# A planned attention and feed-forward kernel: g as two rows, another first order of loads and squares, double score steps from pair 6

## The chip, the cores and the metric

The kernel runs on one NeuronCore of a Trainium2 chip. The metric is the device time of one execution in microseconds (us); lower is better. Before the change three runs gave 427.59, 427.06 and 425.68 us, median 427.06. The engines are called as in the profile: PE (TensorE, matmuls; PEld its weight loads), ACT (ScalarE), DVE (VectorE), POOL (GpSimd) and SP (SyncE, which here issues DMAs). A name with q, such as SPq, is the engine's instruction queue.

## The reference

Attention over 8 batches, 12 heads, 448 tokens and 64 columns a head, with q and k normalised, and behind it a gated feed-forward layer on all 3584 tokens:

```python
def rmsnorm(x, g):
    rms = np.sqrt(np.mean(x * x, axis=-1, keepdims=True) + 1e-06)
    return x / rms * g
q_n, k_n = (rmsnorm(q, g_q), rmsnorm(k, g_k))
scores = scale * np.matmul(q_n, k_n.transpose(0, 1, 3, 2))
attn = np.exp(scores - max); attn = attn / sum
x = np.matmul(attn, v), heads side by side          # 3584 x 768
h = x @ w_in                                        # 768 x 2048
out = (h * np.clip(h + 3.0, 0.0, 6.0) / 6.0) @ w_out  # 2048 x 768
```

## The kernel before

**Units of work.** Two heads make a pair: 6 pairs a batch, 48 in all (HP = 6, NPAIR = 48). A head's 448 tokens are three tiles of 128 and a rest of 64; the rests of a pair's two heads lie together in a fourth tile.

**The way of a pair.** Its q, k and v are loaded from HBM (`load_main`, `load_rest`) into `qk_st` and `v_st`. `square` (L373 on ACT, L375 on POOL) and `sums` (L378, DVE) give the sums of squares; `rstd` (L389, L391, ACT) turns them into the factor 1/rms by a logarithm and an exponential; `normalize` (L399 for pairs 0 to 3, L401 behind) multiplies q or k by it, on POOL, or on DVE for q of pairs 0 and 1 (`DN`), in which case the factor lies in a PSUM bank. Each of the two is then turned so that the 64 columns of a head lie on the partitions: by PE transposes (L418, L421, L425) up to pair 11, by a DMA from pair 12 on (TD). `put_k` (L351) and `put_q` (L439 on DVE, L437 on ACT) copy them into `qkT`; `put_q` multiplies by `gprime`, which holds g_q x g_k / 8 on 128 partitions. `make_g` (L596, L598, ACT) computes it from two loads of 64 numbers to 64 partitions (`load_g`, L592, issued on SP).

**Scores.** `score` (L448) has four steps a pair: three *half steps*, one for each full tile, in which each head's matmul uses one half of PE's rows (the profile shows 64*128, x2), and a *rest step* with one matmul over all rows. `expo` (L463, ACT) writes the exponentials into `eD` (half steps) and `eR` (rest step). `weigh` (L480) multiplies them with `vaug`, the bf16 v with a column of ones, into the bank `av`; `divide` (L490 to L499, DVE) divides by the sum, and `x_out` with `put_x` (L508 to L525) turns the result into `xT`, a batch's x with the 768 columns on partitions.

**Feed-forward.** For each batch `h_mm` (L528) makes 16 tiles of h, six matmuls each; `relu` (L534, ACT) and `gate` (L539, DVE) write `gT`; `y_mm` (L547) makes the output rows, `y_copy` (L351) brings them to SBUF and `y_store` out. w_in comes in eight blocks and w_out in four, one DMA each on POOL's queue (L363), as bf16.

**PSUM.** Eight banks: units 0 and 1 are two banks wide (`sc`, used for scores), 2, 3 and 4 one bank (`ps`), and one is `av`.

**Order.** Nothing is scheduled while it runs: a planner (class `Plan`) plays the kernel through before it is built, and writes out each engine's instructions in the order in which it began them. An operation (`add`) has a key (lower goes first), one or more ways (engine and estimated ns), and what it depends on. Where there are several ways, the estimate is multiplied by a price for its engine (`FIRST` before 45 us, `PRICE` behind). DMAs have an estimated size and landing, with `SLOW`, `BEGIN`, `LATE` and `AHEAD` as allowances, and at most eight are under way. PE takes attention work first, except where a running credit, fed by `share`, hands it to feed-forward items. The engines then work strictly in that order, so an instruction that waits holds up all behind it on its engine.

**What the prediction touches.** The first DMAs: k of pair 0 on SP, q of pairs 0 and 1 on ACT, then the two g loads, k of pair 1, k and q of pairs 2, 3, all on SP; behind them v of pairs 0, 1, v of 2, 3, then k, q and v of 4, 5. The first weight block waits for v of 2, 3. `steps` issues score steps; below pair PB = 12 each by itself, from there on two half steps together (a double), which needs both units 0 and 1. Loads of pairs below MB = 12 (`dense` rows, seven tokens to a partition) take two DMAs, those behind one. `hold` is a one-element memset on POOL that keeps a load back until an earlier pair is normalised.

Of the kernel before, what the change touches and what calls it, by code (L numbers as in the profile page):

```python
# [26 lines left out]
class Op:  # L27


    def __init__(self, key, ways, deps, lag=0, size=0, want=None, cell=None):  # L30
        self.key, self.ways, self.lag, self.size = key, ways, lag, size
        self.want, self.cell, self.gives, self.calm = want, cell, [], None
# [12 lines left out]
class Plan:  # L45
# [8 lines left out]
    UNITS = 5  # L54

    def __init__(self, share):
        self.free = {e: 0.0 for e in ("PE", "ACT", "DVE", "POOL", "SP")}
        self.known, self.todo = [], 0
# [5 lines left out]
    def add(self, key, ways, deps=(), lag=0, size=0, hold=False, want=None, cell=None):  # L64
        op = Op(key, ways, deps, lag, size, want, cell)
        op.left += hold
        op.subs = 0
# [15 lines left out]
    def item(self, lane, place, count, ns, fn, deps, want):  # L83
# [6 lines left out]
        return it  # L90

# [62 lines left out]
    def begin(self, op, engine, ns, fn, now, banks):  # L154
        if banks is not None:
            op.cell["b"] = banks
            for b in banks:
                self.users[b] = list(op.gives)
# [15 lines left out]
    def run(self):  # L174
        now = 0.0
        while self.todo or self.row or any(self.lanes.values()):
            self.flow(now)
            soon = [t for t in self.free.values() if t > now]
# [5 lines left out]
            best = {}  # L184
            for op in self.known:
# [3 lines left out]
                if op.calm is not None and (self.backlog("SP", "ACT") > op.calm[0] + 3000 or self.backlog("POOL") > op.calm[1]):  # L189
                    continue  # L190
                engine, ns, fn = min(op.ways, key=lambda w: max(self.free[w[0]], now) + w[1] * ((self.FIRST if now < self.UNTIL else self.PRICE).get(w[0], 1.0) if op.key[0] >= 0 else 1.0))
                if self.free[engine] <= now and (engine not in best or op.key < best[engine][0].key):
                    if op.subs and not self.room(op, engine, now):
                        continue
                    banks = self.banks_for(op, now, soon) if op.want else None
                    if op.want is None or banks is not None:
                        best[engine] = (op, ns, fn, banks)
            if self.free["PE"] <= now and ("PE" not in best or self.credit < 0):
                if self.row:
                    best["PE"] = (self.row[0], *self.row[0].ways[0][1:], None)  # L200
                else:
                    pick = self.next_item(now, soon)
                    if pick:
# [5 lines left out]
                        best["PE"] = (self.row[0], *self.row[0].ways[0][1:], banks)  # L209
            if not best:  # L210
                now = min(soon)
            for engine, (op, ns, fn, banks) in best.items():
# [5 lines left out]
                else:  # L218
                    self.known.remove(op)
# [8 lines left out]
def kernel(  # L228
# [32 lines left out]
    DENSE, PD, MB = 2 * NT + 1, 4, 12  # L261
# [10 lines left out]
    gq_t = const.tile([P, 1], FP32, name="gq_t")  # L272
    gk_t = const.tile([P, 1], FP32, name="gk_t")
# [30 lines left out]
    plan = Plan(share=(1.4, 1.0, 0.45, 3.0, 0.42, 5.0, 0.4))  # L304
# [139 lines left out]
    def score(p, i, u):  # L444

        qkT = qkT_r[p % NK]
        for h, rows in enumerate((lo, hi) if i < NT else (slice(0, P),)):
            nc.tensor.matmul(  # L448
                out=bank(u, h)[:, 0:S], lhsT=qkT[rows, 0, i * P:(i + 1) * P], rhs=qkT[rows, 1, 0:S],
# [3 lines left out]
    def expo(p, i, u):  # L453
# [4 lines left out]
        else:  # L458
            e, src = eD_t[:, (NT * p + i) % NED], unit_r[u]
            parts = ((e[:, 0:2 * FULL].rearrange("p (h c) -> p h c", h=2), src[:, :, 0:FULL]),  # L460
                     (e[:, 2 * FULL:].rearrange("p (n c) -> p n c", n=3)[:, 0:3:2], src[:, :, FULL:S]))
        for out, in_ in parts:
            nc.scalar.activation(out=out, in_=in_, func=EXP, bias=0.0, scale=1.0)  # L463

    def e_part(p, i, h, j):

        e = eR_t[:, p % NER] if i == NT else eD_t[:, (NT * p + i) % NED]
        heads = 1 if i == NT else 2
        c = h % heads * FULL + j * P if j < NT else heads * FULL + h * REST
# [115 lines left out]
    def clear_e(eng):  # L585
        eng.memset(none[:], 0.0)
        eng.memset(eR_t[:, :, S:W4], 0.0)
        eng.memset(eD_t[:, :, 2 * FULL + REST:2 * FULL + 2 * REST], 0.0)

    def load_g(eng):  # L590
        for dst, src in ((gq_t, g_q), (gk_t, g_k)):
            eng.dma_start(out=dst[lo, :], in_=src.rearrange("(p o) -> p o", o=1))  # L592
# [9 lines left out]
    NFAST = 12  # L602
    CALM = (3000, 100), (5000, 1000)
    SC, ANY = [(0,), (1,)], [(4,), (3,), (1,), (0,), (2,)]
# [7 lines left out]
    ff_banks = [(4,), (3,), (2,)]  # L612
# [27 lines left out]
    def h_item(b, f):  # L640
        deps = [w_ops[f * P // WC]] + px[HP * b:HP * b + HP]
        deps += y_ops.get(b - 2, [])[-1:] + (y_rest.get(b - 1, []) if b % 2 == 0 else [])
        it = plan.item("h", b + f / NFT, NKT, 189, lambda kt, m: h_mm(b, f, kt, m), deps, lambda: ff_banks)
# [3 lines left out]
    def h_early(f):  # L647
        cell, ops = {}, []
        for kt in range(NKT):
            ops.append(add((kt + 2, 2), [("PE", 189, lambda kt=kt: h_mm(0, f, kt, cell["b"][0]))],  # L650
                           [px[kt], at(ops, kt - 1), w_ops[f * P // WC]] + [px[HP - 2]] * (kt == 0), 165,
                           want=any_of((2,), (3,)) if kt == 0 else None, cell=cell))
# [3 lines left out]
    def y_item(b, t, c, n, place):  # L656
        part = c // YC
        deps = [*w_ops[NWI + part * NFT // WR:NWI + (part + 1) * NFT // WR], *gates[b], *(gates[b - 1] if t == NT else [])]
        it = plan.item("y", place, NFT, 163 * n // YC, lambda f, m: y_mm(b, t, c, n, f, m), deps, lambda: ff_banks)
# [35 lines left out]
    YLAG, EARLY = 0.3, 1  # L695

    W_AFTER, LA, VL = 2, 3, 1.2
    DN = ((0, 1), (1, 1))
    MG, EACH = 10, 0.5
    V0, V2, LATER, AHEAD = 2.5, 0.8, -1, 3000  # L700
# [20 lines left out]
    def clear_slots(p):  # L721

        op = add((p - 4, 4), [("POOL", 900, lambda: clear(G, slice(p % NS, p % NS + 2))),
# [19 lines left out]
    def hold(p):  # L743

        cell = qk_st[0:1, 0, p % NS, 0, 0, 0:1]
        held[p] = [add((0, p), [("POOL", 80, lambda: nc.gpsimd.memset(cell, 0.0))], norms[p - (4 if p < 18 else LA)] + norms.get(p - NS, []))]

    def load(a, p, main, rest, rank, aq=nc.sync, qq="SP"):
        if main:
            op = plan.dma((p + rank, a), 2 if PD * (a < 2) <= p < MB else 1, main * 560 * (1.13 if a < 2 and p < PD else 1), lambda: load_main(aq, a, p, main), slot_free(a, p, main) + held.get(p, []), queue=qq)  # L750
# [8 lines left out]
    def load_half(a, p, rest, half, rank, aq=nc.sync, qq="SP"):  # L759
        op = plan.dma((p + rank, a + 0.1), 1, rest * (280 if a == 1 else 140),  # L760
# [7 lines left out]
    def stats(p, st):  # L768
# [4 lines left out]
        srcs = [landed[0][p], landed[1][p]]  # L773
# [191 lines left out]
```

## Time and profile before

| | |
|---|---|
| Median of three runs | 427.06 us |
| Profiled execution, time | 427.18 us |
| Profiled execution, span from first to last instruction | 425.4 us |
| Granted TensorE clock, mean | 1.000 |
| Read from HBM, written | 45.61 MB, 11.01 MB |

| PE group | line | count | busy us | mean ns |
|---|---|---|---|---|
| h matmuls, 448 columns | L528 | 768 | 172.3 | 353 |
| y matmuls, 384 columns (and 192) | L547 | 912 | 169.1 | 323 |
| half steps, 64 rows | L448 | 288 | 43.7 | 361 |
| rest steps | L448 | 48 | 17.3 | 361 |
| weighing | L480 | 1392 | 86.9 | 194 to 223 |

A matmul's busy time runs on after the next one has begun, so the sums of the table overlap; what a matmul costs is read from the distance between starts. In the timeline each line is a start, a length, an engine, a line of the kernel and an operation, with neighbours of one kind merged (x6); behind it in brackets stands the idle time of the engine just before and what ended it. In the list of waits, each line names who waited for whom, the total, the count and the longest.

### The profile page before, as it was taken

How to read it: one execution, taken by the hardware profiler on the slowest of the kernel's cores; microseconds unless marked ns; L12 is line 12 of the kernel's file. 1: busy time of each engine (PE TensorE's matmuls, PEld its weight loads, DVE VectorE, ACT ScalarE, POOL GpSimd, SP SyncE). 2: the span in 40 equal slices, each digit the busy share in tenths (PEclk: the TensorE clock that was granted, in tenths of full speed). 3: DMA queues.
4: the chain of work that ended last, by engine and by line, in shares of the span. 5: the costliest groups of instructions: out<-in, count | busy, mean ns of one | idle time of the engine just before them, and what ended most of it. 6: DMA issues, size and time to landing. Idle time of an engine off the chain costs nothing.

```text
span 425.4 us, 9409 instructions
## 1 busy us (share of the span) xinstructions
PE 407.6 (96%) x3646; PEld 232.0 (55%) x3646; DVE 212.0 (50%) x434; ACT 291.3 (68%) x687; POOL 205.0 (48%) x220
## 2 busy tenths in 40 slices
PE   0888999999999999999999999999999999999996
PEld 0455565555565555555555555555556555555564
DVE  5666887627454565556535675464433432042100
ACT  4799988777868889888887897788663333243211
POOL 5889775773657685685675666784100000000000
PEclk9999999999999999999999999999999999999999
DMA  7999999998899999999499996973311300100121
GB/s 216 195 207 212 181 241 233 161 193 191 185 209 212 209 212 192 224 198 253 111 203 213 219 185 146 223 192 62 85 54 39 86 2 37 75 0 39 74 76 74
DMA packets 128285, 65.11 MB, mean 153 GB/s; under 512 B 78320, under 2 KB 124784, under 8 KB 128240
## 3 DMA queue, kind: packets, MB, share of 16 engines
q1 hardware_dynamic: 117520, 57.76, 63.5%
q0 software_dynamic: 10432, 6.29, 11.0%
q8 instruction: 28, 0.46, 0.5%
q10 hardware_dynamic: 288, 0.46, 0.3%
q14 instruction: 17, 0.14, 0.1%
HBM read 45.61 MB, written 11.01 MB: 133 GB/s over the span
## 4 chain that ended last, share of the span: by engine, by line
PE 91%; ACT 3%; DMA 2%; DVE 2%; SPq 1%; POOL 0%; issue 0%; ACTq 0%; POOLq 0%
PE ps L547 35%; PE ps L528 34%; PE av L480 11%; PE sc L448 10%; ACT eD L463 2%; DMA qk_st<-in_q_dram 2%; PE ps L425 1%; DVE ssq L378 1%; ACT eR L463 0%; PE ps L418 0%; ACT sq L373 0%; SPq L331 0%; DVE gT L539 0%; SPq L592 0%; DVE xn L496 0%
## 5 line engine op out<-in xcount | busy, mean ns | idle before, releaser
L528 PE MATMUL ps<-xT,w_in_sb 128*128 128x448 bf16 x768 | 172.3, 353 | 0.1
L547 PE MATMUL ps<-w_out_sb,gT 128*128 128x384 bf16 (+1 forms) x912 | 169.1, 323 | 0.0
L463 ACT ACTIVATE eD<-sc 128x768 bf16<-128x768 f32 (+1 forms) x288 | 137.1, 555 | 23.0 <-PE sc L448 20.3
L539 DVE SCALAR_TENSOR_TENSOR gT<-t_sb,ps 128x448 bf16<-128x448 f32 x128 | 79.0, 619 | 103.6 <-ACT t_sb L534 102.4
L401 POOL TENSOR_TENSOR qkn<-qk_st,rstd 128x512 bf16<-128x512 f32 x88 | 89.3, 1041 | 49.7 <-ACT rstd L391 47.2
L547 PEld LDWEIGHTS <-gT 128*128 128x128 bf16 x912 | 82.8, 98 | 53.8 <-issue 7.4
L528 PEld LDWEIGHTS <-w_in_sb 128*128 128x128 bf16 x768 | 68.1, 98 | 58.2 <-issue 9.9
L534 ACT ACTIVATE t_sb<-ps 128x448 f32<-128x448 f32 x128 | 70.6, 553 | 33.1 <-PE ps L528 30.3
L375 POOL TENSOR_TENSOR sq<-qk_st 128x1024 f32<-128x1024 f32 (+2 forms) x47 | 78.5, 1682 | 16.6 <-DMA qk_st<-in_q_dram 11.1
L480 PEld LDWEIGHTS <-eD 128*128 128x128 bf16 x1152 | 53.2, 98 | 22.7 <-issue 5.0
L448 PE MATMUL sc<-qkT 64*128 64x448 bf16 (+1 forms) x336 | 60.9, 361 | 2.9 <-ACT eD L463 2.2
L378 DVE TENSOR_REDUCE ssq<-sq 128x16 f32<-128x1024 f32 (+2 forms) x50 | 57.9, 1162 | 10.5 <-POOL sq L375 5.1
L480 PE MATMUL av<-vaug,eD 128*128 128x65 bf16 x1152 | 59.6, 194 | 0.0
L351 ACT COPY y_sb<-ps 128x384 f32<-128x384 f32 (+1 forms) x43 | 20.3, 472 | 55.2 <-PE ps L547 54.8
L351 POOL CAST vaug<-v_st 128x512 bf16<-128x512 f32 x32 | 19.6, 617 | 40.6 <-PE av L480 27.7
L463 ACT ACTIVATE eR<-sc 128x448 bf16<-128x448 f32 x96 | 31.8, 390 | 8.6 <-PE sc L448 8.4
L448 PEld LDWEIGHTS <-qkT 64*128 64x128 bf16 (+1 forms) x336 | 14.9, 94 | 29.1 <-issue 24.5
L437 ACT ACTIVATE qkT<-qkT,gprime 128x448 bf16<-128x448 bf16 x36 | 24.3, 676 | 0.5 <-DMA qkT<-qkn 0.5
L490 DVE RECIPROCAL rden<-av 128x7 f32<-128x7 f32 x48 | 9.7, 201 | 29.8 <-PE av L480 29.8
L496 DVE TENSOR_TENSOR xn<-av,rden 128x384 bf16<-128x384 f32 x42 | 23.4, 557 | 1.6 <-DVE rden L490 0.2
L351 DVE COPY y_sb<-ps 128x384 f32<-128x384 f32 x14 | 7.8, 557 | 27.9 <-PE ps L547 27.9
L480 PEld LDWEIGHTS <-eR 128*128 128x128 bf16 x240 | 16.5, 98 | 7.7 <-issue 2.6
(60 smaller groups left out, 146.5 us busy)
## 6 DMA issues: line engine op xcount, KB each, us to landing
qk_st<-in_k_dram SPq DMA_DIRECT2D x18, 384.0 KB, 4.0
qk_st<-in_q_dram SPq DMA_DIRECT2D x18, 384.0 KB, 4.8
v_st<-in_v_dram SPq DMA_DIRECT2D x18, 384.0 KB, 5.5
out_dram<-y_sb SPq DMA_DIRECT2D x17, 384.0 KB, 2.5
out_dram<-y_sb SPq DMA_DIRECT2D x21, 192.0 KB, 3.2
w_in_sb<-in_moe_w_in_dram POOLq DMA_DIRECT2D x8, 384.0 KB, 7.8
w_out_sb<-in_moe_w_out_dram POOLq DMA_DIRECT2D x4, 768.0 KB, 10.0
v_st<-in_v_dram SPq DMA_DIRECT2D x12, 192.0 KB, 7.8
```

Source lines behind the costliest of these rows:

```text
L351: (eng.copy if eng is nc.scalar else eng.tensor_copy)(out=out, in_=in_)
L375: eng.tensor_tensor(out=sq, in0=x, in1=x, op=A_MULT)
L378: nc.vector.tensor_reduce(out=packed(p, ssq_r[:, p % NR, a]), in_=packed(p, sq_r[m % 2][:, a]), axis=mybir.AxisListType.X, op=A_ADD,)
L401: eng.tensor_tensor(out=qkn_r[p % NQ][:, a].rearrange("p t h d -> p h t d"), in0=qk_st[:, a, p % NS], in1=by[:, a].rearrange("p (h t) -> p ...
L437: eng.activation(out=out, in_=src, func=COPY, scale=gprime[:])
L448: nc.tensor.matmul(out=bank(u, h)[:, 0:S], lhsT=qkT[rows, 0, i * P:(i + 1) * P], rhs=qkT[rows, 1, 0:S], start=True, stop=True,)
L463: nc.scalar.activation(out=out, in_=in_, func=EXP, bias=0.0, scale=1.0)
L480: nc.tensor.matmul(out=av_ps[:, c:c + n], lhsT=e_part(p, i, h, j), rhs=va[:, i].rearrange("p h d -> p (h d)")[:, h * W:h * W + n], start=f ...
L528: nc.tensor.matmul(out=bank(m)[:, 0:S], lhsT=w_in_sb[:, kt, f * P:(f + 1) * P], rhs=xT[:, kt, b % NX, x_slot(b)], start=(kt == 0), stop=(k ...
L534: nc.scalar.activation(out=t[:], in_=bank(m)[:, 0:S], func=RELU, bias=0.5, scale=1.0 / 6.0,)
L539: nc.vector.scalar_tensor_tensor(out=gT[:, f, (b % 2) * S:(b % 2 + 1) * S], in0=t[:], scalar=1.0, in1=bank(m)[:, 0:S], op0=A_MIN, op1=A_MULT,)
L547: nc.tensor.matmul(out=bank(m)[:, 0:n], lhsT=gT[:, f, c0:c0 + P], rhs=w_out_sb[:, f, c:c + n], start=(f == 0), stop=(f == NFT - 1),)
```

## The change

The parts, as the diff has them:

- **g.** The two vectors are loaded as two rows on one partition, issued on ACT's queue behind q of pair 1. DVE multiplies them into one row that holds the product twice (`mix_g`), a matmul of that row with a single 1.0 puts the 128 numbers on 128 partitions (`turn_g`), and DVE copies them to `gprime` (`put_g`). `clear_e` sets the 1.0.
- **First order.** With g off SP, k of pair 1 is SP's second DMA. The squares of pair 1 depend, for the planner, on pair 0's first factor (`AFTER_R0`), those of pair 2 on pair 0's first normalisation (`AFTER_N0`). v of pairs 0 to 3 ranks later (3.5 and 2.5 behind its pair).
- **Score steps.** PB goes from 12 to 6. Each step is now an operation of its own; those behind the first are forced to follow it at once. Rest steps may use any unit. The columns of `eD` are in another order: head 0 with its rest, zeros, head 1's rest, head 1. The code also has steps in threes and a way to hold weighing back as filler; with P3 = 48 and FILL = -3000 (the credit ends at -2000) neither takes place.
- **Which engine.** Both normalisations of pairs 2 to 6 go to DVE. Prices and keys are other ones; from pair 10 instead of 12 the squares of q and k are one POOL instruction.
- **Loads.** MB goes from 12 to 6; rests of pairs 4 to 7 come two pairs at a time. Loads may be issued a pair earlier (`hold`), and the planner's estimates for DMAs differ.

```diff
-    PRICE, FIRST, UNTIL = {"POOL": 0.5, "ACT": 1.5, "DVE": 1.5}, {"POOL": 0.6, "ACT": 1.5, "DVE": 0.9}, 45e3
+    PRICE, FIRST, UNTIL = {"POOL": 0.5, "ACT": 2.0, "DVE": 1.5}, {"POOL": 0.5, "ACT": 1.7, "DVE": 1.0}, 45e3
-    SLOW, BEGIN = 0.88, 10.3e3
-    STEADY, SLACK, LATE = 100e3, 500, {"load": 3000, "turn": 2000}
+    SLOW, BEGIN = 1.6, 3.6e3
+    STEADY, SLACK, LATE = 70e3, 500, {"load": 3500, "turn": 2000}
...
-    DENSE, PD, MB = 2 * NT + 1, 4, 12
+    DENSE, PD, MB = 2 * NT + 1, 4, 6
...
-    plan = Plan(share=(1.4, 1.0, 0.45, 3.0, 0.42, 5.0, 0.4))
+    plan = Plan(share=(1.6, 1.0, 0.45, 3.0, 0.42, 4.0, 0.4))
...
     def load_g(eng):
-        for dst, src in ((gq_t, g_q), (gk_t, g_k)):
-            eng.dma_start(out=dst[lo, :], in_=src.rearrange("(p o) -> p o", o=1))
-
-    def make_g():
-
-        nc.scalar.activation(out=gq_t[lo, :], in_=gq_t[lo, :], func=COPY, scale=1.0 / 8.0)
-        for rows in (lo, hi):
-            nc.scalar.activation(out=gprime[rows, :], in_=gq_t[lo, :], func=COPY, scale=gk_t[lo, :])
+        for i, src in enumerate((g_q, g_k)):
+            eng.dma_start(out=g_row[:, i], in_=src.rearrange("(o d) -> o d", o=1))
+
+    def mix_g():
+
+        nc.vector.scalar_tensor_tensor(
+            out=g_two[:], in0=g_row[:, 0:1].to_broadcast([1, 2, D]), scalar=1.0 / 8.0,
+            in1=g_row[:, 1:2].to_broadcast([1, 2, D]), op0=A_MULT, op1=A_MULT,
+        )
+
+    def turn_g(u):
+        nc.tensor.matmul(out=bank(u)[:, 0:1], lhsT=g_two.rearrange("o h d -> o (h d)"), rhs=unit[:], start=True, stop=True)
+
+    def put_g(u):
+        nc.vector.tensor_copy(out=gprime[:], in_=bank(u)[:, 0:1])
...
-    NFAST = 12
-    CALM = (3000, 100), (5000, 1000)
-    SC, ANY = [(0,), (1,)], [(4,), (3,), (1,), (0,), (2,)]
+    NFAST = 10
+    CALM = (3000, 500), (5000, 1000)
+    SC, ANY = [(0,), (1,)], [(2,), (3,), (4,), (1,), (0,)]
+    RESTS = [(0,), (1,), (3,), (2,), (4,)]
...
-    YLAG, EARLY = 0.3, 1
+    YLAG, EARLY = 0.12, 1
...
-    DN = ((0, 1), (1, 1))
+    DN = ((0, 1), (1, 1), 2, 3, 4, 5, 6)
...
-        srcs = [landed[0][p], landed[1][p]]
+        srcs = [landed[a][p] + [r0[a] for a in AFTER_R0.get(p, ())] + [x for a in AFTER_N0.get(p, ()) for x in norms[0][a:a + 1]] for a in range(2)]
...
-            lg = plan.dma((0.1, 0), 2, 300, lambda: load_g(nc.sync))
             load(0, 1, 1, 0, 0)
             load(1, 1, 1, 0, 0, nc.scalar, "ACT")
+            lg = plan.dma((1, 1.2), 2, 40, lambda: load_g(nc.scalar), queue="ACT")
...
-            load(2, 0, 2, 4, V0)
-            lv = load(2, 2, 2, 0, V2)
+            load(2, 0, 2, 4, 3.5)
+            lv = load(2, 2, 2, 0, 2.5)
...
-            mg = add((-3, 0), [("ACT", 600, make_g)], [lg, *norms[0][1].deps.values()])
+            cell = {}
+            m1 = add((-3, 0), [("DVE", 150, mix_g)], [lg, *squares[:2]])
+            m2 = add((-3, 0), [("PE", 200, lambda c=cell: turn_g(c["b"][0]))], [m1, zero], 165, want=any_of(*ANY), cell=cell)
+            mg = add((-3, 0), [("DVE", 90, lambda c=cell: put_g(c["b"][0]))], [m2])
+            m2.gives = [mg]
...
-            want = [(0, 1)] if len(todo) == 2 else SC
-            key = (-1, todo[0][0])
-            op = add(key, [("PE", ns, run)], deps + last_step, 165,
-                     want=any_of(*want), cell=cell)
+            want = [(*THIRD, 0, 1)] if third else [(0, 1)] if len(todo) == 2 else SC if half[0] else RESTS
+            ns = [189 + half[0] * (101 * (n == 0) + 101 * (n == len(todo) - 1)) for n in range(len(todo))]
+            ops = [add((-1, todo[0][0]), [("PE", ns[n], lambda n=n, p=p, i=i: run(n, p, i))], deps + last_step if n == 0 else [], 165,
+                       hold=n > 0, want=any_of(*want) if n == 0 else None, cell=cell if n == 0 else None) for n, (p, i) in enumerate(todo)]
+            op = ops[0]
+            op.chain = ops[1:]
...
-            PB = 12
+            PB, P3 = 6, 48
```

More of the change, by code (lines that the diff above doesn't have):

```diff
@@ L90, in item, with burst_due @@
         return it
+    def burst_due(self):
+        return self.credit >= self.DUE and any(op.parts and op.time <= self.now + self.SOON for op in self.known)
     def banks_for(self, op, now, soon):
@@ L209, in run @@
                         best["PE"] = (self.row[0], *self.row[0].ways[0][1:], banks)
+                    elif spare and "PE" not in best:
+                        best["PE"] = spare
+            if self.free["PE"] <= now and self.forced:
+                op = self.forced.pop(0)
+                best["PE"] = (op, *op.ways[0][1:], None)
             if not best:
@@ L894, in steps @@
-                op.gives.append(e)
+                if third and n == 0:
+                    e = [add((p, 0), [("ACT", (440, 490)[h], lambda p=p, i=i, h=h: expo_head(p, i, h, THIRD[h]))], [ops[n], old]) for h in range(2)]
+                    for h in range(2):
+                        op.parts[THIRD[h]].append(e[h])
+                else:
+                    e = [add((p, 0), [("ACT", 850 if i < NT else 545, lambda p=p, i=i, c=cells[n]: expo(p, i, c["b"]))], [ops[n], old])]
+                    (op.parts[n - 1] if third else op.gives).append(e[0])
```

114 lines of the change are left out of this document (69 added, 45 removed).

## The prediction

> **What bounds the kernel now.** I read the page first (parts 1 and 2), then who waited for whom on PE, the timeline of the first 40 us, and last the busy time by stretches.
>
> ```profile
> PE 407.6 (96%) x3646; PEld 232.0 (55%) x3646; DVE 212.0 (50%) x434; ACT 291.3 (68%) x687; POOL 205.0 (48%) x220
> ...
> PE   0888999999999999999999999999999999999996
> ...
> DVE  5666887627454565556535675464433432042100
> ACT  4799988777868889888887897788663333243211
> ```
>
> PE is the bound: after the first four slices (10.6 us each) it never pauses. A busy PE isn't yet a useful one, so two things can shorten the time: what happens before PE is full, and PE time that the order itself wastes. First the waits of PE (us in all, times, longest):
>
> ```profile
> PE ps L418 <- POOL qkn L399: 11.1, 2, 9.8
> PE sc L448 <- ACT eD L463: 2.2, 6, 0.5
> ```
>
> PE lost 11.1 us to POOL's normalised k of pairs 0 and 1. The timeline (start, length) says why:
>
> ```profile
> 1.20 0.57 SPq L592 DMA_DIRECT2D gq_t<-in_g_q_dram  x1
> 1.81 0.59 SPq L592 DMA_DIRECT2D gk_t<-in_g_k_dram  x1
> 2.44 1.06 SPq L331 DMA_DIRECT2D qk_st<-in_k_dram  x2
> ...
> 5.68 0.21 ACT L391 ACTIVATE rstd<-lnv 128x7 f32<-128x7 f32 x1
> ...
> 7.90 0.93 POOL L375 TENSOR_TENSOR sq<-qk_st 128x448 f32<-128x448 f32 x1 [2.54 <-DMA qk_st<-in_k_dram]
> ...
> 8.79 0.93 POOL L399 TENSOR_TENSOR qkn<-qk_st,rstd 128x448 bf16<-128x448 f32 x1
> ...
> 11.83 0.93 POOL L375 TENSOR_TENSOR sq<-qk_st 128x448 f32<-128x448 f32 x1 [1.22 <-DMA qk_st<-in_q_dram]
> ...
> 12.72 0.94 POOL L399 TENSOR_TENSOR qkn<-qk_st,rstd 128x448 bf16<-128x448 f32 x1
> ```
>
> The factor for pair 0's k is ready at 5.89, but POOL works in order and stands 2.54 us before the square of pair 1's k, whose load was issued behind the two loads of g. Only then does it normalise pair 0 (8.79), and PE starts at 9.78. The same happens again at 11.83: a square of pairs 2, 3, waiting for their q, stands ahead of pair 1's normalisation at 12.72, and PE stops until 13.71.
>
> From there ACT sets the pace. By stretches (PE, PEld, DVE, ACT, POOL busy):
>
> ```profile
> 20.00:30.00 10.00, 8.66 (x141) 5.79 (x140) 7.62 (x18) 9.94 (x27) 7.89 (x11) 1.00 1.17 226
> 30.00:40.00 10.00, 8.56 (x132) 5.97 (x129) 6.94 (x15) 8.97 (x26) 9.92 (x13) 1.00 1.24 194
> 40.00:50.00 10.00, 10.00 (x100) 5.48 (x100) 7.19 (x15) 9.80 (x27) 6.21 (x8) 1.00 1.27 225
> ```
>
> Feed-forward matmuls begin at 37.78, when batch 0's six pairs are done; from then on PE is full. The last view is a stretch of PE's timeline with a single score step and one with a double:
>
> ```profile
> 46.78 0.35 PE L528 MATMUL ps<-xT,w_in_sb 128*128 128x448 bf16 x1
> 47.06 0.36 PE L448 MATMUL sc<-qkT 64*128 64x448 bf16 x2
> 47.36 1.31 PE L528 MATMUL ps<-xT,w_in_sb 128*128 128x448 bf16 x6
> ...
> 205.42 0.92 PE L528 MATMUL ps<-xT,w_in_sb 128*128 128x448 bf16 x4
> 206.27 0.55 PE L448 MATMUL sc<-qkT 64*128 64x448 bf16 x4
> 206.76 1.50 PE L528 MATMUL ps<-xT,w_in_sb 128*128 128x448 bf16 x7
> ```
>
> Feed-forward matmuls start 0.19 apart (6 take 1.31 with a last one of 0.35). A single step thus costs (47.36 - 46.78) - 0.19 = 0.39 us, a double (206.76 - 205.42) - 4 x 0.19 = 0.58: merging two saves 0.20 us of PE.
>
> **The change part by part.** The sum stands against the profiled execution: 427.18 us, of which 425.4 span and 1.78 around it; the median of the runs shown is 427.06, so 0.12 less.
>
> *Doubles from pair 6 instead of 12.* Pairs 6 to 11 have 3 half steps each, 18 singles; they become 9 doubles. 9 x 0.20 = 1.8 us of PE, in a stretch where PE is full: **-1.8**.
>
> *g, first loads, order of the squares.* Pair 0's factor is ready at 5.89; with its normalisation next on POOL (0.93) PE starts at about 6.9, which is 2.85 earlier. Pair 1's k goes out on SP at 1.2 instead of 2.44; with the 5.4 us to landing that it has now (7.85 less 2.44) it lands at 6.6. Then POOL's square, after pair 0's normalisation, 6.9 to 7.8; sum 0.62; factor 0.42; normalisation 0.94; with hops PE turns pair 1 at 10.1 instead of 13.71: -3.6. Ends: -0.5, if the load of pair 1 only shares the bandwidth it had; -4.8, if the six us between the first score steps of pairs 0 and 1 (11.41 and 17.44) also shrink to the mean 3.92 of pairs 1 to 5. I take **-3.5**. The g path: two row loads on ACT's queue, landing 3.8 to 5.5 after issue at about 2, then a DVE product (nearest row 0.19, the reciprocal of 7), a one-row f32 matmul (no such row; 0.24 to 0.56, between the zero transposes at 10.17 and the score step at 17.44) and a DVE copy (0.2). Ready at 6.5 to 8.6, against the first use at about 8.3; nothing, up to +1.0 because DVE's sums and q's normalisation queue behind a product that waits for its load. The three ACT instructions that go (0.19 and 0.60) lay in idle ACT time: nothing.
>
> *Normalisation of pairs 2 to 6 on DVE, squares and casts priced towards POOL.* Off POOL: 4 x 0.94 + 6 x 1.04 = 10.0 us. Onto DVE: 4 x 0.61 + 6 x 0.65 (0.61 scaled from 448 to 512 columns, with start-up) = 6.3. ACT's four squares between 12 and 37 us (2.31) can move to the freed POOL. ACT's pace of 3.92 a pair is 3.15 of exponentials and 0.77 of the rest, so up to -2.2 over pairs 1 to 5; but DVE, 15.2 busy of the 22 us from 15 to 37, rises to 20 or 21, and its copies into qkT stand in the same queue: up to +2. I take **nothing**, both ends kept.
>
> *Loads.* From pair 6 a main load is one DMA instead of two: 9 SP issues of 0.62 less, and three stores of batch 1. Nothing, since SP is on the ending chain with 1%; without that cover -0.5. The v of pairs 2, 3 moves behind k and q of pairs 4, 5 (seven issues, 4.3 us), and the first weight block waits for that v: 15.33 becomes up to 19.6. It lands 7.8 later, ten us ahead of its first use. The eighth block, issued at 54.68, is needed near 73 (68 after the shift): some 1 us of cover is left if all eight shift by 4.3. The extra memset, the other exponential layout (same shapes) and the changed choice of engine for y copies (ACT 0.48, DVE 0.56, one of them at the very end): nothing, within 0.1.
>
> *What is late next.* Batch 0's feed-forward has 96 matmuls. By 73.69, 89 of them were done; the other seven end at about 75.0, and the last x of batch 1 is written at 74.50 + 0.38 = 74.88. So PE stays fed now with 0.15 us to spare, and all that is gained before is kept only if batch 1's attention also ends 5.3 us sooner. ACT is busy 32.9 of the 36.7 us from 37 to 73.7; squares of pairs 10, 11 that leave it (4 x 0.53) help, but a double takes both score banks and makes ACT wait. Give-back between 0 and 5.3; I take **+0.7**, nearer to zero because after the shortening ACT would need 30.8 of 34.9 us. After that point 18 us of batch 1's matmuls cover the wait for the second weight.
>
> Sum: -1.8 - 3.5 + 0.7 = -4.6; 427.18 - 4.6 = **422.6**.
>
> One rule is weighed here. Two score matmuls took 0.55 at 14.28 and 0.36 from 19.72 on, though the granted clock reads 1.00 in every stretch: early PE work ran at about half speed. By the Trainium skill ("TensorE: Matmul & The Clock Gate", Part 1) the PE clock is halved until some 3.4 us of sustained work; this trace shows about 5.6 us from 13.71, and doesn't show the halving in its clock column. By that rule an earlier start with pauses stays slow, and the sum would be that of rival C.
>
> **Rivals.** *B, deeper*: ACT's relief counts in full, the ramp gives 4.8, nothing is given back: 427.18 - 1.8 - 4.8 - 2.2 = 418.4. For it: POOL has 10 us less to do; against: DVE at 95%.
>
> *C, the ramp stays long*: PE starts at 6.9 but runs at half speed till 19 as now, or DVE becomes the bound from 15 to 37. The 2.85 us are then worth half at best, and 0.7 net of DVE's queue: 427.18 - 1.8 - 0.7 = 424.7. For it: the slow rows up to 18.4; against: PE would have work without the present gaps at 11.9 and 12.8.
>
> *D, it does nothing that counts*: batch 1 ends when it does now, because its loads and ACT, busy 19.65 of 20 us from 40 to 60, set it; PE then idles at the end of batch 0's matmuls for all it won: 427.2.
>
> *E, slower*: the doubles' waits. Where doubles stand now, ACT's exponentials waited 20.0 us for score steps in 32 waits, 0.62 each. Nine of them at pairs 6 to 11, 5.6 us, where ACT has 0.35 us free, less 2.1 for the squares that leave it: batch 1's x comes 3.5 later, 430.6. It decides from the point where the doubles cost ACT more than 2.1 us and no single-bank step fills the gap; against it, the rest step may now use any bank.
>
> **How the numbers follow.** My forecast 0.56 (own range 420.6 to 424.7: the ramp between 1.4 and 4.8, give-back 0 to 0.7), B 0.12, C 0.12, D 0.10, E 0.10. Half a per cent, 2.1 us, is about what a measurement of this kernel can tell from no change. Faster holds my forecast, B and half of C: 0.74; same the other half and D: 0.16; slower E: 0.10. The range from 418.4 to 427.3 reaches from B to D and leaves out E and half of B, 0.16.
>
> **What would show it.** PE's first matmul near 6.9 and pair 1's transposes near 10; POOL's second square behind its first normalisation; no wait of PE for POOL's L399 above 7 us; feed-forward beginning near 34; groups of four score matmuls from pair 6 on; the last x of batch 1 near 70 with no PE gap ahead of batch 1's matmuls; PE's busy time lower by about 2. I'd be wrong if PE waits between 40 and 80 us, for ACT's exponentials or for a weight block, or if DVE runs full from 12 to 34 and pairs still follow 4 us or more apart.

## The result and the profile after

The changed kernel is slower: a median of 429.1 us (14 runs, 427.53 to 430.88) against 426.9 (425.04 to 427.80) for the kernel before on the same chip, a ratio of 1.0054 with a 95% interval of 1.0037 to 1.0072. The forecast was 422.6 with a range of 418.4 to 427.3, so its sign was wrong and the measured time lies above its range. The profiled execution took 427.80 us, of which 425.3 is span, against 427.18 and 425.4.

The page of the kernel after, busy time by engine and in slices of 10.6 us:

```profile
PE 406.9 (96%) x3648; PEld 233.6 (55%) x3648; DVE 235.7 (55%) x477; ACT 272.9 (64%) x647; POOL 197.9 (47%) x215
...
PE   2979999999989999999999999999999999999996
...
DVE  7986878438356476464762852835734443343321
ACT  5989797667667886887868749969688232132100
```

PE's first slice has work now, and ACT is busy 18 us less in all. But the third slice shows a 7, and the twelfth an 8 where PE was full before. The waits of PE, and the start of the timeline of the kernel after:

```profile
PE ps L626 <- DVE g_two L620: 7.1, 1, 7.1
PE ps L534 <- DVE xn L516: 2.9, 4, 1.5
PE sc L466 <- ACT qkT L455: 2.7, 2, 1.4
PE ps L466 <- DVE gT L562: 0.9, 1, 0.9
```

```profile
5.87 0.94 POOL L417 TENSOR_TENSOR qkn<-qk_st,rstd 128x448 bf16<-128x448 f32 x1 [0.62 <-ACT rstd L409]
...
6.76 0.98 POOL L393 TENSOR_TENSOR sq<-qk_st 128x448 f32<-128x448 f32 x1
...
7.58 0.58 PE L436 MATMUL ps<-identity,qkn 64*64 64x64 bf16 x14
...
9.34 0.94 POOL L417 TENSOR_TENSOR qkn<-qk_st,rstd 128x448 bf16<-128x448 f32 x1
...
9.95 1.02 PE L466 MATMUL sc<-qkT 128*128 128x448 bf16 x3 [1.37 <-ACT qkT L455]
```

The start is as forecast: pair 0's normalisation stands ahead of the second square on POOL, and the 11.1 us of waits for POOL are gone. PE's first matmul is now the one that turns g, at 7.09 (the 7.1 us "wait" for it is only the time before any work). Pair 0's k follows at 7.58. Pair 1's transposes start at 10.90.

Busy time by stretches (PE, PEld, DVE, ACT, POOL), the stretches shown of before and two later ones, of the kernel after and then, for the later ones, of before:

```profile
20.00:30.00 10.00, 7.27 (x108) 4.84 (x104) 8.79 (x19) 9.05 (x24) 4.14 (x7) 1.00 1.26 241
30.00:40.00 10.00, 8.99 (x122) 5.61 (x123) 8.42 (x17) 8.90 (x26) 9.85 (x12) 1.00 1.22 262
40.00:50.00 10.00, 10.00 (x118) 6.24 (x117) 7.18 (x17) 9.07 (x22) 9.41 (x11) 1.00 1.04 203
...
90.00:100.00 10.00, 9.12 (x95) 5.20 (x92) 6.45 (x14) 7.51 (x18) 5.45 (x3) 1.00 1.20 240
120.00:130.00 10.00, 8.64 (x94) 5.48 (x92) 5.33 (x8) 6.29 (x17) 7.16 (x4) 1.00 1.10 252
```

```profile
90.00:100.00 10.00, 10.00 (x88) 5.79 (x86) 6.05 (x14) 6.48 (x16) 4.30 (x3) 1.00 1.27 193
120.00:130.00 10.00, 10.00 (x97) 5.91 (x96) 5.20 (x12) 6.64 (x18) 5.59 (x5) 1.00 1.19 186
```

Batch 1's stretch (40 to 50) is full, as it was. The loss stands where the prediction didn't look: at 90 to 130 us, in the middle of the kernel, PE now pauses. Two of the pauses, in the timeline of the kernel after:

```profile
92.52 0.67 ACT L455 ACTIVATE qkT<-qkT,gprime 128x448 bf16<-128x448 bf16 x1 [1.11 <-DMA qkT<-qkn]
...
93.65 0.62 DVE L562 SCALAR_TENSOR_TENSOR gT<-t_sb,ps 128x448 bf16<-128x448 f32 x1 [2.35 <-ACT t_sb L557]
...
94.32 0.35 PE L466 MATMUL ps<-qkT 128*128 128x448 bf16 x1 [0.88 <-DVE gT L562]
...
127.17 0.67 ACT L455 ACTIVATE qkT<-qkT,gprime 128x448 bf16<-128x448 bf16 x1 [3.67 <-DMA qkT<-qkn]
...
127.89 0.36 PE L466 MATMUL sc<-qkT 64*128 64x448 bf16 x2 [1.36 <-ACT qkT L455]
```

The first line of each group is ACT standing still for a q that a DMA turns (1.11 and 3.67 us). At 127.89 PE waits for that q itself. At 94.32 the way is longer: behind ACT's waiting copy stands the relu of a feed-forward tile, behind that DVE's gate, and a rest step of scores waits for the bank (`ps`) that the gate is to free.

To see where time goes I add up, for every matmul, the distance to the start of the next less what its kind needs when matmuls follow closely (0.189 us for 448 columns, 0.162 for 384, and so on, 0.098 for a change between 64 and 128 rows). I call the sum *PE time beyond need*:

| | before | after |
|---|---|---|
| first matmul starts | 9.78 | 7.09 |
| beyond need, up to 40 us | 9.2 | 9.8 |
| first h matmul of batch 0 | 37.78 | 35.53 |
| first h matmul of batch 1 | 75.24 | 71.22 |
| beyond need, 40 to 70 us | 0.65 | 0.80 |
| beyond need, 70 to 130 us | 0.76 | 3.48 |
| beyond need, behind 130 us | 2.22 | 3.01 |
| last matmul starts | 421.94 | 421.86 |
| time outside the span | 1.78 | 2.5 |

The changed kernel was 4.0 us ahead when batch 1's feed-forward began. Of these, 3.5 go in PE's time beyond need behind 70 us (6.5 against 3.0) and some 0.4 in ways that these sums don't show; the last matmul starts where it did, and 0.7 more lie outside the span.

These two executions differ by 0.6 us only, the medians by 2.2. The one of before was late for its kind: on the four chips of the experiments, runs of before with a mean clock of 0.998 or more have medians of 425.5 to 426.3 us, and this one took 427.18; the five such runs of the changed kernel have 427.8, the four of its repeat 428.8. So about 1 us of the lead of 4.0 belongs to that execution and not to the change.

### The profile page after: what moved, and what is told of

The parts are those of the page before. It is cut to its first block, busy times and chain, and to the rows that moved or that the text cites. A ratio compares the mean times of both kernels' runs of the same rounds, so it can differ in the third digit from the quotient of the medians.

```text
span 425.3 us, 9434 instructions
## 1 busy us (share of the span) xinstructions
PE 406.9 (96%) x3648; PEld 233.6 (55%) x3648; DVE 235.7 (55%) x477; ACT 272.9 (64%) x647; POOL 197.9 (47%) x215
## 4 chain that ended last, share of the span: by engine, by line
PE 83%; DVE 7%; DMA 3%; ACT 2%; SPq 2%; issue 1%; POOL 0%; ACTq 0%; DVEq 0%
PE ps L570 32%; PE ps L551 32%; PE av L503 10%; PE sc L466 7%; DVE ssq L396 3%; DMA qkT<-qkn 2%; DMA qk_st<-in_q_dram 1%; DVE gT L562 1%; PE ps L466 1%; ACT eD L482 1%; DVE xn L516 1%; DVE xn L519 1%; SPq L541 1%; DVE xn L522 0%; PE ps L443 0%
## 5 line engine op out<-in xcount | busy, mean ns | idle before, releaser
L551 PE MATMUL ps<-xT,w_in_sb 128*128 128x448 bf16 x762 | 168.9, 353 | 0.1
L393 POOL TENSOR_TENSOR sq<-qk_st 128x1024 f32<-128x1024 f32 (+2 forms) x49 | 82.4, 1694 | 93.2 <-DMA qk_st<-in_q_dram 54.2
L562 DVE SCALAR_TENSOR_TENSOR gT<-t_sb,ps 128x448 bf16<-128x448 f32 x127 | 77.5, 620 | 68.9 <-ACT t_sb L557 67.8
L551 PEld LDWEIGHTS <-w_in_sb 128*128 128x128 bf16 x768 | 69.2, 98 | 57.6 <-issue 7.3
L419 POOL TENSOR_TENSOR qkn<-qk_st,rstd 128x512 bf16<-128x512 f32 x82 | 83.4, 1039 | 8.9 <-ACT rstd L409 8.7
L369 DVE COPY y_sb<-ps 128x384 f32<-128x384 f32 (+1 forms) x52 | 28.6, 550 | 82.6 <-PE ps L570 79.6
L466 PE MATMUL sc<-qkT 64*128 64x448 bf16 (+1 forms) x305 | 48.5, 360 | 3.6 <-ACT qkT L455 2.7
L466 PEld LDWEIGHTS <-qkT 64*128 64x128 bf16 (+1 forms) x336 | 14.1, 95 | 23.9 <-issue 18.0
L482 ACT ACTIVATE eR<-ps 128x448 bf16<-128x448 f32 (+1 forms) x62 | 21.9, 437 | 0.4 <-PE ps L466 0.4
L369 POOL CAST vaug<-v_st 128x512 bf16<-128x512 f32 x28 | 16.9, 619 | 8.8 <-PE sc L466 3.3
L503 PE MATMUL av<-vaug,eR 128*128 128x130 bf16 (+1 forms) x240 | 19.4, 212 | 0.0
```

The costliest lines, as they stand in the source:

```text
L369: (eng.copy if eng is nc.scalar else eng.tensor_copy)(out=out, in_=in_)
L393: eng.tensor_tensor(out=sq, in0=x, in1=x, op=A_MULT)
L419: eng.tensor_tensor(out=qkn_r[p % NQ][:, a].rearrange("p t h d -> p h t d"), in0=qk_st[:, a, p % NS], in1=by[:, a].rearrange("p (h t) -> p ...
L466: nc.tensor.matmul(out=(bank(u[h]) if isinstance(u, tuple) else bank(u, h))[:, 0:S], lhsT=qkT[rows, 0, i * P:(i + 1) * P], rhs=qkT[rows, 1 ...
L503: nc.tensor.matmul(out=av_ps[:, c:c + n], lhsT=e_part(p, i, h, j), rhs=va[:, i].rearrange("p h d -> p (h d)")[:, h * W:h * W + n], start=f ...
L551: nc.tensor.matmul(out=bank(m)[:, 0:S], lhsT=w_in_sb[:, kt, f * P:(f + 1) * P], rhs=xT[:, kt, b % NX, x_slot(b)], start=(kt == 0), stop=(k ...
```

## The experiments

Each ran in five rounds; ratios are against the kernel before on the same chip. Letters of theories are those of the expectation they stand in.

**Repeats.** Both kernels again, with the same work.

> The kernel before once more, for the spans and clocks of its single runs. All theories: 426.9 us. If the granted clock of 0.996 that 10 of 14 runs of the changed kernel show belongs to the chip, it shows here in a like share of runs; if it belongs to the changed order of work, here every run is at 1.000. The time outside the span, 1.78 us in the profiled run of before and 2.5 after, should come out 1.8 here if it belongs to the kernel.

> The changed kernel once more, beside the others on one chip. 429.1 us if nothing else varies. The time outside the span was 2.1 to 2.5 us in its 14 runs and 1.73 to 1.85 in all runs of before and of e2 and e3: if that belongs to the changed program it is 2.3 again and 0.55 us of the loss is not in any engine's work; if it belonged to the other chip it is 1.8, and the time some 428.4.

Before again: 1.0004 (0.9984 to 1.0025). After again: 428.99 us, 1.0070 (1.0043 to 1.0096), so the loss is real. Two things had to be learnt from these. The first matmul of before started at 8.61 in this profiled execution and at 9.78 in the first one, and the first half step with 0.36 us instead of 0.56 came at 16.92 instead of 19.72: the starts of one kernel differ by 1 us and more, and the baseline of the prediction was a late one. And a granted clock of 0.996 or less instead of 1.000, which I had first put down to the changed order, appears in 8 of the 12 runs of the kernel before as well; between these two kernels it says nothing. In three kernels below (doubles alone, doubles with two-unit rest steps, normalisations back on POOL), whose PE pauses for 2.6 us and more, no run is above 0.996, so there it is part of the loss.

### The score steps

The kernel before with doubles from pair 6 and nothing else:

```diff
-            PB = 12
+            PB = 6
```

> The kernel before with one number changed: double score steps from pair 6 instead of 12. The prediction's term: nine merges of 0.20 us each, 425.1 us. Theory P (the place of the score steps): a double takes both score units, ACT is starved between doubles, batch 1's attention ends later and PE runs out of batch 0's feed-forward matmuls ahead of it: several us of PE waiting between 60 and 80 us, 429 to 432 us.

433.67 us, 1.0166 (1.0138 to 1.0195): the worst of all. Waits of PE, and busy time in stretches of 2 us, of this kernel:

```profile
PE ps L508 <- DVE xn L499: 3.8, 2, 2.6
```

```profile
70.00:72.00 2.00, 0.61 (x9) 0.33 (x9) 1.05 (x4) 1.96 (x6) 2.00 (x3) 0.97 1.22 190
72.00:74.00 2.00, 1.79 (x16) 0.86 (x17) 0.55 (x2) 1.28 (x2) 2.00 (x4) 0.50 1.74 191
...
76.00:78.00 2.00, 0.00 (x0) 0.00 (x0) 1.94 (x5) 0.31 (x1) 1.98 (x2) 1.00 1.39 94
```

ACT and POOL are full at 70 to 72 (1.96 and 2.00 of 2) while PE has run out of batch 0's work, and the granted clock falls to 0.50 in the stretch behind. The last x of batch 1 is there at 80.2 instead of 74.9. This is rival E of the prediction in its place, only larger: 5.3 us later where it had 3.5. Its mechanism is seen in part: from 38 to 82 us ACT's exponentials wait 3.2 us for score steps (1.0 before), where the rival had 5.6.

The kernel after, with rest steps bound to the two score units again, and then with single steps instead of doubles:

```diff
-    RESTS = [(0,), (1,), (3,), (2,), (4,)]
+    RESTS = SC
```

> The changed kernel with its doubles from pair 6, but rest steps in the two score units only. Theory P: the single banks no longer relieve the doubles, so batch 1 ends late and PE waits some 4 us between 60 and 80 us, while the waits behind 140 us (246 and 321) go: 430 to 431 us. Theory D: no such wait at 60 to 80, 429 us, with the waits at 93 and 126 as they are.

```diff
-            PB, P3 = 6, 48
+            PB, P3 = 12, 48
```

> The changed kernel with doubles only from pair 12, but rest steps still in any unit (e2 had both undone: 426.2 us, no PE wait behind 60 us above 0.1). If the rest steps in the feed-forward banks cost PE time by themselves, there are waits behind 90 us again, 2 to 4 us in all, and 428 to 429. If only the doubles of pairs 6 to 11 brought the waits, it is as fast as e2: 426.

And both, so that all of the change is there except its score steps:

> The changed kernel with the score steps as before: doubles from pair 12 only, rest steps in the two score units only. Theory P expects the PE waits after 40 us (5.7 us of PE time beyond what its matmuls need, against 2.5 before) to go back to some 2.5, and the gain of the first 40 us (2.1 us) to stay, so 424.5 to 425.5 us although the 1.6 us of the doubles are given up. Theory D (loads and turning DMAs that SP issues in another order land late) expects the waits at 93 and 126 us to stay: 430 us.

| ratio to before | rest steps in the two score units | in any unit |
|---|---|---|
| singles in batch 1 | 0.9997 (0.9976 to 1.0018) | 1.0042 (1.0017 to 1.0066) |
| doubles in batch 1 | 1.0072 (1.0041 to 1.0103) | 1.0070 (1.0043 to 1.0096) |

The entry for the changed kernel is the repeat's; its first measurement was 1.0054. The old score steps give back the whole loss, 426.2 us, but not the gain of the start that theory P counted on (424.5 to 425.5). (The 5.7 and 2.5 us in that expectation were summed too low; the table above has 7.3 and 3.6 for everything behind 40 us. With the old steps it is 3.3.) Doubles with rest steps in two units take 429.0 us, below the 430 to 431 of theory P, and make PE stop at the end of batch 1, as in the kernel with doubles alone:

```profile
72.00:74.00 2.00, 0.00 (x0) 0.00 (x0) 1.88 (x5) 0.41 (x1) 1.31 (x2) 0.87 0.50 112
```

Rest steps in any unit heal that and cost elsewhere: with singles they make the kernel slower by about half a per cent (429.5 us), since there was nothing to heal. PE's waits at 93 and 127 us stand in neither kernel that has one of the two edits alone; they need both. So the two edits don't add up, and neither pays by itself.

### The start

The kernel before with the new first order only: g as rows, the order of the first squares, v later, and the planner's allowances for the first DMAs. (This kernel and the next keep the new code's form: the columns of `eD` in the other order, each score step an operation of its own, and a third bank for batch 0's first h tiles.)

```diff
+    r0, AFTER_R0, AFTER_N0 = {}, {1: (0,)}, {2: (0,)}
...
-    SLOW, BEGIN = 0.88, 10.3e3
+    SLOW, BEGIN = 1.6, 3.6e3
```

> The kernel before with the g rows, the first order of loads and squares, the later v of pairs 0 to 3 and the planner's two constants for the first loads; nothing else of the change (normalisations, prices, score steps, load sizes as before). The prediction's ramp term: 3.5 us less, 423.4. Theory R (what starts PE sooner is taken back before 40 us, since ACT, POOL and DVE are nearly full from 12 to 36 and set the pace of the first six pairs): PE starts at about 7.2 but feed-forward begins no more than 1.5 us sooner, 425 to 426.

425.73 us, 0.9970 (0.9953 to 0.9987): a gain that holds to the end, 1.3 us, not 3.5. And g alone, its rows, product, matmul and queue:

```diff
-            lg = plan.dma((0.1, 0), 2, 300, lambda: load_g(nc.sync))
+            lg = plan.dma((1, 1.2), 2, 40, lambda: load_g(nc.scalar), queue="ACT")
```

> The kernel before with g as two rows, turned by the matmul and copied by DVE, its loads on ACT's queue, and so pair 1's k second on SP; no other edit of order. The prediction's account: POOL still squares pair 1's k ahead of pair 0's normalisation, which now waits less, so 1 to 1.5 us of e5's gain comes from here: 425.5 to 426.5. If the gain lies in the order of the squares alone, no change: 426.8.

1.0010 (0.9993 to 1.0028): nothing. The g path costs nothing, as the prediction had it, but pair 1's earlier k brings nothing by itself either, against the first account in that expectation. The gain of 1.3 us needs the order of the squares, the later v or the planner's allowances; these weren't parted. Next, the kernel with old score steps and the normalisations of pairs 2 to 6 back on POOL, and the same kernel with the old prices of engines before 45 us:

```diff
-    DN = ((0, 1), (1, 1), 2, 3, 4, 5, 6)
+    DN = ((0, 1), (1, 1))
```

> e2 (score steps as before) with the normalisations of pairs 2 to 6 back on POOL. Rival C of the prediction, DVE as the bound of the ramp: PE's idle time from 20 to 35 us, 3.8 us in e2, falls by 1.5 to 2 and the time to 424.5. If DVE wasn't the bound, POOL's 10 us of normalisations come back into the way and the time is as e2 or up to 2 us longer: 426 to 428.

```diff
-    PRICE, FIRST, UNTIL = {"POOL": 0.5, "ACT": 2.0, "DVE": 1.5}, {"POOL": 0.5, "ACT": 1.7, "DVE": 1.0}, 45e3
+    PRICE, FIRST, UNTIL = {"POOL": 0.5, "ACT": 2.0, "DVE": 1.5}, {"POOL": 0.6, "ACT": 1.5, "DVE": 0.9}, 45e3
```

> e2 (changed kernel, score steps as before) with the engine prices of before for the first 45 us, which put more squares and casts on ACT and fewer on POOL. If POOL's share held the ramp in e2 (PE without work for 17.4 us in the first 40), 1 us less: 425. If ACT is the ramp's bound, longer: 427.

POOL back: 1.0068 (1.0048 to 1.0089), with a wait of 2.7 us for POOL's normalisation, from 26.7 to 29.4, and 3.4 us at half clock behind it. DVE doesn't become a bound that loses, as rival C had it; with this order its help is worth 0.7% (1.0068 against 0.9997). The old prices give 0.9972 (0.9956 to 0.9989), level with the first order alone: the new prices seem to cost some 1 us (0.9997 against 0.9972, with intervals that overlap), where the prediction had nothing. These two, the first order alone and the old score steps with the old prices, are the best versions found, both about 0.3% faster than the kernel before.

### The waits behind 70 us

The kernel after, with rest steps in any unit only where they are needed, below pair 12:

```diff
-            want = [(*THIRD, 0, 1)] if third else [(0, 1)] if len(todo) == 2 else SC if half[0] else RESTS
+            want = [(*THIRD, 0, 1)] if third else [(0, 1)] if len(todo) == 2 else SC if half[0] or todo[0][0] >= 12 else RESTS
```

> The changed kernel with one condition more: rest steps may use any unit only below pair 12, where the doubles need relief; from pair 12 on the two score units alone. If the rest steps in feed-forward banks are what brings PE's waits behind 72 us (some 3.5 us more than before), these fall to those of before, batch 1 stays early (first matmul of batch 1 near 71), and the time is 425.5 to 426.5. If the waits are those of loads and turning DMAs that come late, they stay: 428.5 to 429.

428.14 us, 1.0021 (1.0002 to 1.0040). PE's time beyond need behind 130 us falls from 3.0 to 2.0, which is less than before's 2.2; from 70 to 130 us it is still 3.1 (3.5 in the kernel after). So the banks of later rest steps cost some 1 us, and the rest has another cause. On top of it, the planner's spare time for PE from 100 us on instead of from 70:

```diff
-    STEADY, SLACK, LATE = 70e3, 500, {"load": 3500, "turn": 2000}
+    STEADY, SLACK, LATE = 100e3, 500, {"load": 3500, "turn": 2000}
```

> e8 with one planner constant of before as well: the later landing of loads and the slack for PE are reckoned with from 100 us on instead of 70. Theory of the banks: no PE wait behind 40 us beyond those of before, doubles from pair 6 and the early batch 1 kept, 424 to 425, so faster than both kernels. Theory of the late DMAs: with less allowance between 70 and 100 us waits appear there, 428 or more.

1.0057 (1.0032 to 1.0081), worse: one wait of 2.5 us for ACT's exponentials, from 92.8 us, with 3.4 us at half clock behind it. Without spare time the order breaks in this same place. Then, on the first of these two, 2 us more for each transpose by DMA:

```diff
-    STEADY, SLACK, LATE = 70e3, 500, {"load": 3500, "turn": 2000}
+    STEADY, SLACK, LATE = 70e3, 500, {"load": 3500, "turn": 4000}
```

> As the kernel in which rest steps take any unit only below pair 12, and the planner moreover expects each q and k turned by a DMA 4 us late instead of 2. Theory D (the waits at 93 to 128 us come from DMA-turned q that lands later than the planner thinks, with ACT's copy of it in front of exponentials): PE's idle time beyond what its work needs falls behind 40 us from 5.2 to 4 or less, no single wait between 90 and 130 us is above 0.3 us, and the time is 426.5 to 427.3. Rival N (the waits come from ACT's order and the banks of double steps themselves, whatever the turned q does): waits of 0.5 to 0.9 us stay between 90 and 130, and the time is 428 to 429.

427.06 us, 0.9987 (0.9964 to 1.0009), level with before. The waits at 93, 95, 120 and 128 us are gone; in this kernel one of PE's waits is left behind 70 us:

```profile
PE ps L570 <- DVE gT L562: 1.2, 1, 1.2
```

Beyond need, 70 to 130 us come to 2.0 instead of 3.1, and the time outside the span to 1.78 instead of 2.08: 1.4 us together, a third of a per cent, which is the difference of the two ratios. The time is theory D's, its other two signs are not: it expected 4 or less behind 40 us, and it is 5.5 (some 5.9 without this edit, by the same sum), and no wait above 0.3 between 90 and 130, and the wait shown stands at 103 to 104.2. No DMA is in that one: DVE's sums of squares, 1.22 us up to 102.98, stand ahead of the two gates that PE waits for. So the late q explains the four waits, not all of the loss. At last, pairs 12 and 13 turned by PE:

```diff
-    TD, XD, XQ = 12, 12, 6
+    TD, XD, XQ = 14, 12, 6
```

> As the kernel in which rest steps take any unit only below pair 12, with pairs 12 and 13 turned by PE instead of by a DMA. It costs PE about 0.9 us a pair (the transposes of one pair), 1.8 in all, and takes the first two transposes by DMA off SP's queue at 70 to 78 us. Theory D: the waits between 90 and 100 us (1.4 us in two) fall below 0.5 and the loads of the next pairs go out earlier; the time is 428.5 to 429.2, that is at most 1 above the kernel it starts from. Rival N: waits between 90 and 100 stay as they are, the time is 429.8 to 430.5.

428.65 us, 1.0022 (0.9995 to 1.0049), with single runs from 425.3 to 432.7. The time is the one that theory D gave, but by luck: PE turns the two pairs for some 0.9 us in all (16 matmuls more, 0.056 apart), not 1.8, and a wait of 1.3 us is left between 90 and 100. If the pairs are issued in order, it is for the same pair 14, the third that a DMA turns in the kernel it starts from (issued at 79.28, landed at 93.05) and the first one here. The timeline of this kernel has its chain in three lines:

```profile
80.58 5.48 SPq L448 DMA_TRANSPOSE qkT<-qkn  x1
...
95.30 0.67 ACT L455 ACTIVATE qkT<-qkT,gprime 128x448 bf16<-128x448 bf16 x1 [2.07 <-DMA qkT<-qkn]
...
96.01 0.35 PE L466 MATMUL sc<-qkT 128*128 128x448 bf16 x1 [1.33 <-ACT qkT L455]
```

The issue of the transpose holds SP for 5.48 us. Its last piece lands at 95.27, by the semaphore that ACT's copy waits on: 14.7 us after the issue began. The copy begins then, PE behind it. (The next transpose, held from 89.62 to 95.32, is another pair's and lands at 99.74.) In the kernel with 2 us more for each transpose, one is held for 8.54 us from 81.42 and lands at 95.33; ACT copies at 95.92 and hasn't waited. What took the waits away there was the allowance in the order, not a shorter hold.

## Why the prediction was wrong, point by point

**What bounds the kernel**: right. PE is the bound, and all that counted, won or lost, was PE's.

**Doubles, -1.8**: as PE work, right. The last start less the first start and the time beyond need (421.94 - 9.78 - 12.86, and 421.86 - 7.09 - 17.06) is 399.3 before and 397.7 after, 1.6 less. The first of them, in the kernel after, with its neighbours:

```profile
43.71 0.35 PE L551 MATMUL ps<-xT,w_in_sb 128*128 128x448 bf16 x1
44.00 0.55 PE L466 MATMUL sc<-qkT 64*128 64x448 bf16 x4
44.48 0.55 PE L551 MATMUL ps<-xT,w_in_sb 128*128 128x448 bf16 x2
```

Four matmuls in (44.48 - 43.71) - 0.19 = 0.58 us, the price that was taken. What it needs was wrong: the rest steps in other banks, which the prediction named only as a help against rival E, are the price of the doubles, and had no term. By the runs, old score steps against new ones (0.9997 against 1.0054, in the repeat 1.0070), the edit of the score steps costs 2.4 to 3.1 us, with some 1 us of uncertainty, where the prediction had -1.8.

**The start, -3.5**: mis-sized. The places were right (7.09 for 6.9, pair 1 at 10.9 for 10.1, no wait for POOL above 7 us), yet alone it is worth 1.3 us (0.6 to 2.0). Some 1 us was never there, because the baseline's profiled execution began late. And the lead shrinks on the way: 3.3 us at the first score step of pairs 1 and 2 (17.4 to 14.1, 21.4 to 18.1), 1.7 at those of pairs 3 and 5. Between the two repeats it is 1.2 and 0.6 at pairs 1 and 2 (16.24 to 15.00, 19.74 to 19.11). The value lies between the ends that were named, -0.5 and -4.8, and a little short of the -1.4 of the range.

**Half speed**: the first half step with 0.36 us instead of 0.56 comes at 16.42 against 19.72, but at 16.92 in the repeat of before and at 17.46 in that of after. Among the eight kernels whose first matmul starts at 7.1 to 7.3 us it comes anywhere from 15.08 to 18.83. So the end of the slow stretch doesn't follow PE's start, it differs by execution, and the late one of the baseline made the start look dearer than it is. This part of rival C is not settled.

**Normalisation on DVE, 0**: mis-sized. In the changed order it is worth 0.7%, some 3 us (the run with POOL back), more than the 2.2 that were named as its end, though within the uncertainty of some 1.2 us; the prices beside it seem to cost some 1 us. DVE is busy 4.84 of 5 us from 10 to 15. PE's waits for DVE's x come to 2.9 us in the kernel after and to 0.6 with the old score steps, so most of them don't come from the normalisations.

**g path, weights and loads, 0**: right. The rows of g alone change nothing, and no wait of PE names a weight block.

**What is late next, +0.7**: near, for the place it names. Batch 1's feed-forward began 4.0 us sooner, where -1.8 - 3.5 + 0.7 makes 4.6; some 1 us of the 4.0 is the late baseline. Of the signs named for being wrong, PE waiting between 40 and 80 us didn't come. The other came in part: DVE is busy 19.4 of the 22 us from 12 to 34, and pairs 1 to 5 follow 4.3 us apart (14.07 to 31.45, at their first score steps), where before had 3.92 and the kernel with the old score steps has 3.9.

**The step that failed**: the doubles at -1.8 without a term for what they need, and the sentence "After that point 18 us of batch 1's matmuls cover the wait for the second weight". With it everything behind 75 us was taken as unchanged. Loads, keys and banks change there as well, and pairs from 12 on are turned by DMAs that wait their turn on SP. In the two profiles this costs 3.5 us behind 70 us: 1.0 for rest steps in other banks (run), some 1.1 for q that lands later than the order allows for (run and trace), the rest in waits of the same stretch whose parts I didn't separate. Another 0.7 lies outside the span, for which the prediction had no term. Added up by runs: the start gives -1.3 alone, all of the change without its score steps -0.1, the score steps +2.4 to +3.1, together the +2.3 to +3.0 measured. Rival E had the right sign and 430.6, near the median; that is luck, since PE doesn't wait at the end of batch 1 in the kernel as changed, only in the runs with doubles and two-unit rest steps.

## What to carry to other kernels

An order written out beforehand is tuned as a whole: an edit that saves work in one stage must also be priced in the stages behind it, above all where in-order queues hold DMAs with uncertain landing, and "full before" is no cover there. When an edit comes with a second one that makes it bearable, run the two by two table: here neither paid, and the small edit at the start was worth more than all of it. Take the baseline from more than one execution: the one used here was 1 us late. Judge a lead of a few us by when the last stage begins, not by the first instruction.

## What the runs showed of the hardware

**Half clock behind short pauses.** In the profile of the unaltered kernel's repeat, PE paused from about 22.2 to 23.96 for ACT's exponentials; the stretches of 2 us are

```profile
22.00:24.00 2.00, 0.27 (x10) 0.24 (x6) 0.93 (x1) 1.59 (x4) 1.03 (x1) 0.84 1.16 212
24.00:26.00 2.00, 1.69 (x11) 0.79 (x11) 1.97 (x4) 1.97 (x7) 1.33 (x2) 0.50 1.14 220
26.00:28.00 2.00, 2.00 (x25) 1.35 (x23) 0.49 (x2) 1.97 (x6) 2.00 (x3) 0.50 1.44 202
28.00:30.00 2.00, 2.00 (x20) 1.32 (x18) 0.99 (x3) 1.34 (x4) 1.98 (x4) 0.50 1.13 208
```

The granted clock (the column with 0.50) falls to half at 23.37, inside a pause of 1.7 us, and stays there for 6.83 us. In the other profiled executions seven pauses of 1.9 to 3.6 us have a stretch at half clock that begins inside them or up to 1.1 us behind, of 3.41 or 6.83 us; one of 1.9 us has none. Of the pauses up to 1.6 one has such a stretch: 1.2 us, close behind another of 0.7 (at 71 in the kernel with doubles alone). A mean clock of 0.996, as many runs have it, is what one stretch of 3.4 us makes of 425 (0.5 x 3.4 / 425 = 0.004). The Trainium skill ("TensorE: Matmul & The Clock Gate", Part 1) has the clock halved after about 3.4 us of idling. The lengths of the stretches agree with windows of 3.4 us; the pauses that were enough here are shorter.

**A transpose by DMA can hold its queue.** In the kernel after, the issue at 78.65 held SP for 7.92 us, and the loads behind it until 86.62; the shortest for q and k took 1.23. The data landed at 92.50, and ACT's copy at 92.52 waited for them. The kernel with only the new first order has one of 7.61 and loses nothing by it, so it matters only where something is due. What makes an issue long is not shown.

**Time outside the span.** It goes with the program: 1.8 us before, 1.77 to 1.85 in the profiled executions of nine other kernels, 1.99 to 2.07 in three, 2.1 to 2.6 in the runs of the kernel after. No run explains it; it stays open.
